# Row maxima of an attention block: the elementwise output goes back over the PSUM columns that were read

## The chip, the cores and the metric

The kernel runs on one core of a Trainium2 chip. The metric is the device time of one execution in microseconds; lower is better. A core has five engines with a queue each: TensorE (PE in the profile; its weight loads are PEld), VectorE (DVE), ScalarE (ACT), GpSimd (POOL) and SyncE (SP), which here only issues transfers. Each engine works through its own queue in order and waits on semaphores where it needs another's result, or, as will matter here, its own.

## The reference

Four layers in a row, A B A B, on a sequence of 2048 tokens of width 640. Each adds to `x` the output of an attention with 32 heads of 20 columns, taken of the layer-normalized `x`. A is linear attention. B cuts the sequence into four segments of 512 and mixes a causal softmax inside each segment with a memory of the segments before:

```
def _B_ref(x, wq, wk, wv, wo, beta):
    ...
    for s in range(N):                       # N = 4 segments of L = 512
        qs, ks, vs = q[:, :, s], k[:, :, s], v[:, :, s]
        logits = jnp.einsum("bhqd,bhkd->bhqk", qs, ks) * scale + mask
        p = _softmax(logits, axis=-1)
        a_dot = jnp.einsum("bhqk,bhkd->bhqd", p, vs)
        pq = phi(qs)
        num = jnp.einsum("bhld,bhde->bhle", pq, M)
        den = jnp.einsum("bhld,bhd->bhl", pq, z)[..., None] + 1e-6
        o = g * (num / den) + (1.0 - g) * a_dot
        ...
```

The softmax needs the maximum of each row of the masked logits. That maximum is what the changed line computes.

## The kernel before

Two streams of work are woven together: the dense one (layer norms, transposes, projections with split 16-bit weights, the linear attention and the memory) and the attention of the B layers. A planner with rough costs decides in which order their pieces are emitted. TensorE's queue keeps that order exactly (it is the one engine in `MANUAL`); the queues of the others are put in order by the scheduler of the language, from the same emission order and from what it takes to be ready.

The attention of a B layer goes by groups of four heads: eight groups in a segment, four segments, two layers, so 64 groups. Each group runs through three stretches (`STRETCHES`), in which work on the new group is interleaved with the group before and the one before that. What bears on the change:

- `stacks` loads the queries and keys of the group (lines 994 and the like).
- `row_max` (lines 997 to 1016) makes the logits a second time, only for their maxima. For each entry of `MAXES` it takes two PSUM banks, one for each half (`par`) of the partitions that hold the heads, lets TensorE write the products into them (line 1008), and then reduces them on VectorE (line 1015). There are five entries for a group, so 320 pairs of banks in all and 16 maxima for a group, 1024 in all. Three of the five entries hold two pieces of columns: 384 and 128 twice, and 256 and 256 once; two hold one piece of 512.
- Line 1015 is one instruction for the maximum, which adds a 16-bit mask (`maskw`) to the products and takes the largest sum of each row. It has two outputs: the sums themselves, elementwise, which nobody reads, and the maximum, which comes into `mg` by a second instruction that reads the accumulator out. In the profile the first is CUSTOM_DVE_ANT_0 and the second DVE_READ_ACCUMULATOR2_ANT, both at L1015.
- The elementwise output goes into `junk`, a 16-bit tile of 512 columns in SBUF with one buffer, so all 1024 maxima write the same memory.
- `split_max` (lines 1024 and 1025) turns the 16 maxima of a group into a sum of two 16-bit numbers, TensorE transposes these (line 1033), ScalarE copies them (line 1035), and a transfer writes them as two further rows of the queries (line 1038). They are subtracted by the matmul of the scores.
- `scores` (line 1050) makes the logits again, transposed and with the maxima taken off, and ScalarE takes their exponential (line 1054); GpSimd zeroes the triangle (line 1061); `weigh` (line 1077) multiplies with the values, and `normalize` (lines 1090 to 1101) divides.

The eight PSUM banks are taken in turn by everything that TensorE makes (`bank`, tag `ps`, 8 buffers). A bank is given out again when its last reader is done. So a matmul of whichever kind can wait for a maximum, through the bank that the maximum still reads. Other lines that the prediction names: 325 and 330 (transposes and the copy of their low part), 387 and 401 (projections), 428 (a sum of two SBUF tiles), 465 (the memory's quotient), 545 (a running sum), 885 and 893 (the memory's update), 1093 and 1100 (the reciprocal and the product of `normalize`).

Of the kernel before, what the change touches and what calls it, by code (L numbers as in the profile page):

```python
# [23 lines left out]
SEG = 512  # L24
# [118 lines left out]
class Kernel:  # L143
# [855 lines left out]
    def row_max(self, G, todo):  # L999

        nc, bp, qs, ks = self.nc, self.bp, G["qs"], G["ks"]
        bs = [self.bank() for _ in range(2)]
        cost = 0
        for p, i, a in todo:
            n = (i + 1) * P
            for par in range(2):
                r = slice(64 * par, 64 * par + 60)
                nc.tensor.matmul(bs[par][:, a:a + n], qs[r, p, i * P:(i + 1) * P], ks[r, p, :n],  # L1008
                                 start=True, stop=True)
                cost += n * COL  # L1010
        for par in range(2):
            for p, i, a in todo:
                n = (i + 1) * P
                junk = bp.tile([P, SEG], BF16, tag="junk", name="junk", bufs=1)
                nc.vector.tensor_tensor_reduce(junk[:, :n], bs[par][:, a:a + n], self.maskw[:, SEG - n:],  # L1015
                                               1.0, NEG, OP.add, OP.max, G["mg"][:, par, p, i:i + 1])
        return cost

# [346 lines left out]
```

## Time and profile before

| | us |
|---|---|
| median of 3 runs | 1751.35 |
| lowest and highest of them | 1750.96, 1752.2 |
| span of the profiled execution | 1750.1 |
| VectorE busy in it | 1195.0 |
| of that, line 1015 | 499.3 |
| TensorE busy in it (modelled ends) | 1674.0 |

The span goes from the first to the last instruction of one execution. The profile says nothing of what lies around it; the median of the runs is 1.25 us longer. Busy time of TensorE is an upper reading, since the ends of its pipelined matmuls are modelled. A group of instructions is named by its source line, engine, operation and out<-in by the program's names; then come the shapes, the count, the busy time, the mean in ns, and the idle time of its engine in front of it with what ended it.

### The profile page before, as it was taken

Reading aid. Unit: us, or ns where it says so; the run is one execution under the profiler, and the core shown is the slowest. Engines: PE = TensorE matmul, PEld = TensorE weight load, DVE = VectorE, ACT = ScalarE, POOL = GpSimd, SP = SyncE. Lnnn points to the kernel's source line nnn. Section 1 sums busy time; section 2 is a strip of 40 time slices with the busy share of each in tenths; the row PEclk is TensorE's granted clock in tenths of the full one; section 3 lists DMA queues with packets and bytes.
Section 4 is the critical chain, followed back from the end, with each engine's and each line's share of the span. In section 5 each row is a group of like instructions: output and inputs, shape, how many; then the busy total and the mean of one; then the engine's idle time right before and its main releaser. Section 6 shows DMA issues by size and latency. Waiting matters only on the chain.

```text
span 1750.1 us, 36310 instructions
## 1 busy us (share of the span) xinstructions
PE 1674.0 (96%) x13032; PEld 1045.6 (60%) x13032; DVE 1195.0 (68%) x3856; ACT 970.3 (55%) x1818; POOL 519.0 (30%) x982
## 2 busy tenths in 40 slices
PE   6999999999999999999989999999999999999998
PEld 4676666654665566456556777566446545644555
DVE  8645534577787677768864456746888877878773
ACT  5545433357557546667665553333675575666674
POOL 1543350022123312433342211221421432233452
PEclk9999999999999999999999999999999999999999
DMA  7422453422322322361211303433232323223332
GB/s 263 180 109 94 151 187 107 135 70 90 109 69 82 107 86 81 123 204 53 77 43 44 109 31 121 169 103 114 74 106 79 111 80 107 92 82 109 126 118 91
DMA packets 118332, 187.60 MB, mean 107 GB/s; under 512 B 13948, under 2 KB 79612, under 8 KB 115848
## 3 DMA queue, kind: packets, MB, share of 16 engines
q1 hardware_dynamic: 105896, 142.68, 25.2%
q0 software_dynamic: 3040, 21.63, 3.5%
q10 hardware_dynamic: 9216, 20.98, 3.1%
q8 instruction: 103, 1.69, 0.4%
q14 instruction: 77, 0.63, 0.1%
HBM read 106.05 MB, written 78.64 MB: 106 GB/s over the span
## 4 chain that ended last, share of the span: by engine, by line
PE 73%; DVE 13%; ACT 6%; issue 3%; POOL 2%; DMA 2%; SPq 0%; ACTq 0%; DVEq 0%; POOLq 0%
PE ps L401 31%; PE ps L387 16%; PE ps L1077 6%; DVE junk L1015 4%; PE ps L1050 3%; PE ps L325 3%; PE ps L1008 3%; ACT pe L1054 3%; PE ps L566 3%; PE ps L456 3%; PE ps L893 1%; PE ps L1090 1%; PE ps L732 1%; DVE st L344 1%; DVE oT L330 1%
## 5 line engine op out<-in xcount | busy, mean ns | idle before, releaser
L1015 DVE CUSTOM_DVE_ANT_0 junk<-ps,maskw 128x512 bf16<-128x512 f32 (+3 forms) x1024 | 499.3, 488 | 90.5 <-PE ps L1008 30.1
L1054 ACT ACTIVATE pe<-ps,lsc 128x512 f32<-128x512 f32 x640 | 394.6, 694 | 95.9 <-PE ps L1050 92.4
L1061 POOL TENSOR_SCALAR_AFFINE_SELECT pe<-pe 128x256 f32<-128x256 f32 (+1 forms) x640 | 229.7, 366 | 446.5 <-ACT pe L1054 442.0
L401 PEld LDWEIGHTS <-xT 128*128 128x128 f16 x2880 | 280.6, 98 | 114.9 <-issue 10.9
L401 PEld LDWEIGHTS <-oT 128*128 128x128 f16 x1920 | 185.5, 98 | 80.0 <-issue 6.9
L1077 PE MATMUL ps<-pe,v 128*32 128x512 f32 (+3 forms) x2048 | 161.5, 439 | 8.0 <-POOL pe L1061 3.3
L401 PE MATMUL ps<-w_Bo,oT 128*128 128x320 f16 x960 | 141.9, 301 | 1.5 <-ACT pe L1054 0.9
L387 PE MATMUL ps<-xT,w_Bq 128*128 128x512 f16 x600 | 140.1, 379 | 1.7 <-ACT pe L1054 0.8
L1008 PE MATMUL ps<-ks,qs 60*128 60x512 f16 (+3 forms) x1024 | 129.0, 299 | 12.2 <-DVE mg L1015 3.4
L401 PE MATMUL ps<-w_Bv,xT 128*128 128x320 f16 x960 | 139.7, 299 | 0.7 <-ACT v L434 0.7
L387 PE MATMUL ps<-xT,w_Bk 128*128 128x512 f16 x600 | 138.8, 379 | 1.1 <-DVE mg L1015 0.5
L401 PE MATMUL ps<-w_Ak,xT 128*128 128x320 f16 x960 | 136.1, 299 | 0.5 <-ACT r L415 0.5
L1050 PE MATMUL ps<-qs,ks 62*128 62x512 f16 (+3 forms) x1024 | 106.5, 300 | 3.3 <-ACT pe L1054 1.5
L858 DVE SCALAR_TENSOR_TENSOR nat<-ps,nat 128x512 f16<-128x512 f32 x80 | 54.9, 687 | 77.6 <-ACT nat L857 77.5
L427 POOL TENSOR_SCALAR e<-e 128x320 f32<-128x320 f32 (+1 forms) x52 | 82.4, 1584 | 83.4 <-ACT e L423 79.2
L1077 PEld LDWEIGHTS ps<-pe,v 128*32 128x32 f32 x2048 | 63.6, 110 | 65.7 <-issue 43.5
L1008 PEld LDWEIGHTS <-qs 60*128 60x128 f16 x1024 | 50.8, 94 | 82.5 <-issue 55.1
L857 ACT ACTIVATE nat<-ps 128x512 f16<-128x512 f32 x80 | 48.2, 602 | 93.6 <-PE ps L387 73.3
L387 PEld LDWEIGHTS <-w_Bk 128*128 128x128 f16 x600 | 57.4, 98 | 65.2 <-issue 5.3
L387 PEld LDWEIGHTS <-w_Bq 128*128 128x128 f16 x600 | 56.8, 98 | 65.7 <-issue 7.6
L349 POOL TENSOR_TENSOR rs<-rs,mhalf 128x1 f32<-128x1 f32 x48 | 28.3, 590 | 223.8 <-DVE rs L348 215.6
L479 POOL TENSOR_TENSOR xn<-xn,xo 128x320 f32<-128x320 f32 x56 | 48.5, 869 | 139.4 <-ACT xn L478 134.6
(220 smaller groups left out, 2671.9 us busy)
## 6 DMA issues: line engine op xcount, KB each, us to landing
x<-xn ACTq DMA_DIRECT2D x48, 320.0 KB
qs<-qd SPq DMA_DIRECT2D x128, 120.0 KB
ks<-kd SPq DMA_DIRECT2D x128, 120.0 KB
xo<-x SPq DMA_DIRECT2D x48, 320.0 KB
pqi<-pqd SPq DMA_DIRECT2D x32, 320.0 KB
qd<-nat SPq DMA_DIRECT2D x40, 256.0 KB
kd<-nat SPq DMA_DIRECT2D x40, 256.0 KB
x<-in_A_x SPq DMA_DIRECT2D x16, 320.0 KB
```

The costliest lines, as they stand in the source:

```text
L325: nc.tensor.transpose(pt[:, (c - c0) * P:(c - c0 + 1) * P], src[:, c * P:(c + 1) * P], self.ident)
L387: nc.tensor.matmul(p, w[:, c, a, t * P:(t + 1) * P], xT[:, c, b, :], start=k == 0, stop=k == 3 * C - 1)
L401: nc.tensor.matmul(p, xT[:, c, a, i * P:(i + 1) * P], w[:, c, b, n * HN:(n + 1) * HN], start=k == 0, stop=k == 3 * C - 1)
L427: nc.gpsimd.tensor_scalar(e, e, 1.0, eps, op0=OP.min, op1=OP.add)
L456: nc.tensor.matmul(nd[:, lo - k * cut:hi - k * cut], pq[t], mem[:, OFF[t] + lo - a:OFF[t] + hi - a], start=first, stop=True, skip_group_ch ...
L858: nc.vector.scalar_tensor_tensor(nat[:, 1], p, QK_SHIFT, nat[:, 0], op0=OP.mult, op1=OP.subtract)
L1008: nc.tensor.matmul(bs[par][:, a:a + n], qs[r, p, i * P:(i + 1) * P], ks[r, p, :n], start=True, stop=True)
L1015: nc.vector.tensor_tensor_reduce(junk[:, :n], bs[par][:, a:a + n], self.maskw[:, SEG - n:], 1.0, NEG, OP.add, OP.max, G["mg"][:, par, p, i ...
L1050: nc.tensor.matmul(b[:, a:a + n], ks[r, p, j * P:(j + 1) * P], qs[r, p, j * P:], start=True, stop=True)
L1054: nc.scalar.activation(e, b, AF.Exp, scale=self.lsc)
L1061: nc.gpsimd.affine_select(d, d, pattern=pat, compare_op=OP.is_ge, fill=0.0, base=0, channel_multiplier=-1)
L1077: nc.tensor.matmul(G["pv"][32 * h4:32 * h4 + 32, j * P:], v[j][:, h * E1:h * E1 + 32], G.pop((p, par, j)), start=j == 0, stop=j == 2, skip ...
```

## The change

The elementwise output of the maximum goes into the PSUM columns that the instruction reads, as 32-bit, instead of into `junk`, which is no longer used. Nothing reads those columns afterwards. Counts, shapes, mask and maxima stay.

```
             for p, i, a in todo:
                 n = (i + 1) * P
                 junk = bp.tile([P, SEG], BF16, tag="junk", name="junk", bufs=1)
-                nc.vector.tensor_tensor_reduce(junk[:, :n], bs[par][:, a:a + n], self.maskw[:, SEG - n:],
+                nc.vector.tensor_tensor_reduce(bs[par][:, a:a + n], bs[par][:, a:a + n], self.maskw[:, SEG - n:],
                                                1.0, NEG, OP.add, OP.max, G["mg"][:, par, p, i:i + 1])
```

More of the change, by code (lines that the diff above doesn't have):

```diff
@@ L1014, in row_max @@
                 junk = bp.tile([P, SEG], BF16, tag="junk", name="junk", bufs=1)
-                nc.vector.tensor_tensor_reduce(junk[:, :n], bs[par][:, a:a + n], self.maskw[:, SEG - n:],
+                nc.vector.tensor_tensor_reduce(bs[par][:, a:a + n], bs[par][:, a:a + n], self.maskw[:, SEG - n:],
                                                1.0, NEG, OP.add, OP.max, G["mg"][:, par, p, i:i + 1])
```

## The prediction

> **What bounds the kernel now.** I read the engine shares of the page first, then the chain that ended last, then the groups by form, then the timeline of VectorE, and last who waits for the maxima. In the page, the columns are busy time, share of the span and instructions; below it stands the chain by engine, and the two groups of the maxima and the exponentials.
>
> ```profile
> span 1750.1 us, 36310 instructions
> ...
> PE 1674.0 (96%) x13032; PEld 1045.6 (60%) x13032; DVE 1195.0 (68%) x3856; ACT 970.3 (55%) x1818; POOL 519.0 (30%) x982
> ...
> PE 73%; DVE 13%; ACT 6%; issue 3%; POOL 2%; DMA 2%; SPq 0%; ACTq 0%; DVEq 0%; POOLq 0%
> ...
> L1015 DVE CUSTOM_DVE_ANT_0 junk<-ps,maskw 128x512 bf16<-128x512 f32 (+3 forms) x1024 | 499.3, 488 | 90.5 <-PE ps L1008 30.1
> L1054 ACT ACTIVATE pe<-ps,lsc 128x512 f32<-128x512 f32 x640 | 394.6, 694 | 95.9 <-PE ps L1050 92.4
> ```
>
> TensorE leads, but not alone: the chain spends 13% of the span, some 230 us, in VectorE. The line of the maxima is the costliest group of the page and has 4.3% of the chain, 75 us, which the chain in order of time says by line:
>
> ```profile
> by line: PE ps L401 31.0%; PE ps L387 15.7%; PE ps L1077 6.4%; DVE junk L1015 4.3%; PE ps L1050 3.4%; PE ps L325 3.2%; PE ps L1008 3.1%; ACT pe L1054 2.9%; issue 2.9%; PE ps L566 2.7%; PE ps L456 2.7%; PE ps L893 1.4%; PE ps L1090 1.1%; PE
> ```
>
> At 488 ns each, 75 us are 154 of the 1024 maxima; the other 870 run beside TensorE. Windows of the attention (columns: length, busy time and instructions of each engine, granted clock, DMA) tell how full VectorE is there:
>
> ```profile
> 340.00:930.00 590.00, 567.36 (x4685) 343.68 (x4685) 447.47 (x1615) 363.63 (x677) 176.15 (x398) 1.00 0.28 91
> 1190.00:1715.00 525.00, 500.30 (x4147) 287.17 (x4147) 410.13 (x1476) 326.96 (x598) 174.98 (x381) 0.99 0.31 99
> ```
>
> VectorE is busy 858 of these 1115 us (77%), before its own waiting is counted. The clock is full, so nothing here is the throttle's.
>
> **What the change removes: waits of VectorE for itself.** Each row maximum is two instructions, the maximum and an 83 ns readout of its accumulator. All maxima write the one scratch tile, so that each has to wait until the one before it has finished, its readout included. The timeline shows what this costs (start, length, instruction):
>
> ```profile
> 721.12 0.56 DVE L1015 CUSTOM_DVE_ANT_0 junk<-ps,maskw 128x384 bf16<-128x384 f32 x1
> 721.60 0.08 DVE L1015 DVE_READ_ACCUMULATOR2_ANT mg<- 128x1 f32 x1
> 721.72 0.29 DVE L1015 CUSTOM_DVE_ANT_0 junk<-ps,maskw 128x128 bf16<-128x128 f32 x1
> 721.94 0.08 DVE L1015 DVE_READ_ACCUMULATOR2_ANT mg<- 128x1 f32 x1
> 722.16 0.56 DVE L1015 CUSTOM_DVE_ANT_0 junk<-ps,maskw 128x384 bf16<-128x384 f32 x1
> 722.65 0.08 DVE L1015 DVE_READ_ACCUMULATOR2_ANT mg<- 128x1 f32 x1
> 722.76 0.29 DVE L1015 CUSTOM_DVE_ANT_0 junk<-ps,maskw 128x128 bf16<-128x128 f32 x1
> 722.98 0.08 DVE L1015 DVE_READ_ACCUMULATOR2_ANT mg<- 128x1 f32 x1
> 723.21 0.69 DVE L1015 CUSTOM_DVE_ANT_0 junk<-ps,maskw 128x512 bf16<-128x512 f32 x1
> 723.82 0.08 DVE L1015 DVE_READ_ACCUMULATOR2_ANT mg<- 128x1 f32 x1
> 724.05 0.69 DVE L1015 CUSTOM_DVE_ANT_0 junk<-ps,maskw 128x512 bf16<-128x512 f32 x1
> 724.67 0.08 DVE L1015 DVE_READ_ACCUMULATOR2_ANT mg<- 128x1 f32 x1
> 724.67 0.25 DVE L1093 RECIPROCAL rc<-ps 128x16 f32<-128x16 f32 x1
> 724.95 0.49 DVE L1100 TENSOR_TENSOR tmp<-ps,rc 128x320 f32<-128x320 f32 x1
> ...
> 725.59 0.52 PE L325 MATMUL ps<-ident,otok 128*128 128x128 f32 x3 [0.41 <-DVE tmp L1100]
> ```
>
> Three cadences, from the start of a readout to the start of what follows. A reciprocal that waits for nothing recent starts with the readout: 0.00 (724.67). A maximum that waits for this readout alone: 0.11 to 0.12 (721.60, 722.65). A maximum that waits for the readout and also for a new PSUM bank: 0.22 to 0.23 (721.94, 722.98, 723.82), because the second wait needs a separate semaphore instruction, which then stands behind the first. At 725.59 TensorE pays for such a run: it waits for a copy that stands behind six maxima.
>
> The rows that group them:
>
> ```profile
> L1015 DVE DVE_READ_ACCUMULATOR2_ANT mg<- x1024: 76/83/88, 340.1 to 1708.5; 128x1 f32 x171
> L1015 DVEq EVENT_SEMAPHORE  x453: 21/21/21, 346.4 to 1707.6; - x151
> ...
> who waited for it (us, times):
>   PEld ps L325: 4.3, 17
>   PEld L1050: 3.5, 9
>   PE ps L1008: 3.4, 10
> ...
>   PEld ps L893: 1.1, 2
>   PEld L1033: 1.1, 4
>   PE ps L401: 0.8, 2
>   PE ps L387: 0.8, 2
>   PEld ps L885: 0.7, 1
>   PE ps L893: 0.5, 1
> ```
>
> Counted along the whole timeline, 356 maxima have the long cadence behind a readout and 292 the short one; the other 376 stand behind another kind of instruction and lose nothing. To start with the readout instead saves 0.227 and 0.117 us (the exact medians are gaps of 144, 34 and -83 ns from the readout's end).
>
> The changed program, built, says how many waits go. PE's order is the same in all rows. On VectorE 885 maxima carried a wait for VectorE before, 648 of them for the readout directly in front; now 466 do, and only 8 for the one in front. The rest look two or three readouts back, which are done. A pair of banks now reads:
>
> ```
> L1015 ISA ps,mg<-ps,maskw 128x384 [waits PE_49]
> L1015 ISA mg 128x1
> L1015 ISA ps,mg<-ps,maskw 128x384 [waits PE_49]
> L1015 ISA mg 128x1
> L1015 ISA ps,mg<-ps,maskw 128x128 [waits DVE_49]
> L1015 ISA mg 128x1
> L1015 ISA ps,mg<-ps,maskw 128x128 [waits DVE_49]
> ```
>
> Gain on VectorE: 356 x 0.227 + 284 x 0.117 = 81 + 33 = 114 us, or 0.111 us per maximum. On the path only the maxima of the chain count: 154 x 0.111 = 17.1 us. The second reading agrees: the waits of TensorE that a maximum ended add up to 16.2 us in the list above (POOL's left out), in some 50 stalls of 0.3 us, each behind a run of maxima that gets shorter by more than that.
>
> The Trainium skill speaks against this ("VectorE: DVE Perf Modes", The DRAIN you can't avoid): eight copies with a semaphore after each took as long as with one after the last, "the semaphore costs nothing extra here". By that the sum would be zero and the time 1751. The trace does not agree: 0.11 and 0.23 us against 0.00.
>
> **What it adds: order inside a pair of banks.** Three of five pairs in a group hold two parts, 192 in all. VectorE took both parts of the first bank, then both of the second; now the banks alternate, as quoted. By the rows from 721.12 on, the first bank came free after 0.90 us (722.02) and the second after 1.94 (723.06). Without gaps it is 0.48 + 0.48 + 0.22 + 0.08 = 1.26 for the first and 1.48 for the second: 0.36 later, 0.46 earlier. Of some 50 stalls about 15 can hang on such a first bank, at most 5 us; since each earlier pair left VectorE earlier by about as much, I take 2.
>
> **What it adds: the write goes to PSUM as 32-bit.** No VectorE instruction of this kernel writes PSUM, so no row has the price. The nearest are 128x320 instructions with the operands elsewhere:
>
> ```profile
> L465 DVE TENSOR_TENSOR otok<-ps,rc 128x320 f32<-128x320 f32 x48 | 23.3, 488 | 0.4
> L428 DVE TENSOR_TENSOR pk<-e,r 128x320 f32<-128x320 f32 x32 | 15.7, 491 | 35.2 <-POOL e L427 33.9 <-ACT e L423 1.2
> L545 DVE TENSOR_TENSOR z<-z,e 128x320 f32<-128x320 f32 x30 | 15.6, 521 | 0.7
> ```
>
> A first operand in PSUM instead of SBUF is 3 ns cheaper (488, 491); the dearest row is 33 ns above the first. So -3 to +33 ns each; on the chain, 154 times that is 0 to +5 us. I take 0, since PSUM as such does not show in 488 against 491.
>
> **What it moves.** ScalarE, GpSimd and SyncE keep their work; a few normalizations, selects and loads change places with a neighbour, mostly by one exponential, 0.69 us each by the L1054 row. They move both ways; I take 0, and 3 us either way into the range.
>
> **Sum.** -17 + 2 + 0 + 0 = -15 us against the profiled 1750.1, which is 1.25 us under the median of the runs, 1751.35. Forecast: **1736 us**.
>
> **Rivals.**
> *Larger gain, chance 0.12.* The split of the maxima follows the last one of a group, and its consumer waits too, as the list for the tile of the maxima says (its row for the transposes' loads, then its row for the transposes):
>
> ```profile
>   PEld L1033: 15.2, 21
>   PE pm L1033: 4.6, 2
> ```
>
> Were these 20 us gone with the 16, the time would be 1751 - 36 = 1715.
>
> *The write costs more, chance 0.12.* Between 33 and 97 ns each the gain shrinks from 10 us to nothing: 1741 to 1751. The Trainium skill has such a price ("Perfetto Trace Analysis", Optimizing Scalar/DVE Operations): some 60 ns of access overhead on SBUF, 125 on PSUM. By it, 65 ns x 154 = 10 us, an estimate, would leave 1746. The rows of 488 and 491 ns do not show it for reads; no run here shows a write.
>
> *Another wait takes its place, chance 0.10.* Where TensorE no longer waits for maxima it waits for an exponential that was nearly as late: ScalarE is 62% busy in the two windows. For it: line 1054 has 2.9% of the chain. Against: ScalarE itself sat idle 92 us before these for TensorE. Time 1750.
>
> *Slower, chance 0.09.* Reading and writing one bank take turns, so that an element needs two steps. The forms' step is (0.69 - 0.29)/384 = 1.04 ns per element by the timeline; another such step on 320 elements, the mean of 512, 384, 128 and 256 in equal numbers, adds 333 ns. Less the 111 saved that is 222 x 154 = 34 us, plus the 2: 1787. The sign turns at 97 ns each (15 us over 154). Against: a 32-bit write of 0.96 elements per ns is no more than the reading that runs there now.
>
> The forecast as such, gain 9 to 21 us, keeps 0.57.
>
> **Numbers.** Two runs of this kernel differ by some 0.2%, 3.5 us; that bounds "same". Faster: 0.57 + 0.12 + 0.09 of the dearer write = 0.78. Same: 0.09 of the third rival and 0.03 of the second, 0.12. Slower: 0.09 and 0.01 of the third, 0.10. The range goes from the larger gain with a little movement, 1714, to the third rival, 1750; it leaves out the slower case and about a tenth besides.
>
> **What would show it.** Right: maxima that follow a readout start with it (0.00), the semaphore rows at line 1015 fall from 453 to 168, a 128x512 maximum stays at 0.69 us, the waits of TensorE for a maximum halve, and the line's share of the chain falls below 4%. The first step is wrong if 0.11 stays; the write's price is wrong if a 512-column maximum takes over 0.72 us, and the sign if it takes over 0.80; the sum is wrong if VectorE gains its 114 us and TensorE's stalls move to ScalarE.

## The result, and the profile after

The changed kernel takes 1744.6 us (median of 9 runs, 1742.69 to 1745.8) against 1751.15 before on the same chip (9 runs, 1747.26 to 1752.2). The ratio is 0.9963 [0.9954, 0.9973]: a gain of 6.5 us, where 15 were forecast. The profiled execution has a span of 1741.4 us, 8.7 less than that of before. In what follows, "before" and "after" also name the two kernels.

The page of the changed kernel: span, engines, chain by engine, the maxima and their readouts.

```profile
span 1741.4 us, 36031 instructions
...
PE 1668.7 (96%) x13032; PEld 1048.4 (60%) x13032; DVE 1183.8 (68%) x3856; ACT 969.3 (56%) x1818; POOL 518.7 (30%) x982
...
PE 77%; DVE 10%; ACT 6%; issue 2%; POOL 2%; DMA 2%; SPq 0%; ACTq 0%; POOLq 0%; DVEq 0%
...
L1015 DVE CUSTOM_DVE_ANT_0 ps<-ps,maskw 128x512 f32<-128x512 f32 (+3 forms) x1024 | 472.8, 520 | 40.4 <-PE ps L1008 38.1
...
L1015 DVE DVE_READ_ACCUMULATOR2_ANT mg<- 128x1 f32 x1024 | 144.7, 141 | 0.0
```

VectorE's part of the chain falls from 13% to 10%, and the chain by line says that the maxima's own part falls from 4.3% to 1.6% (75 to 28 us):

```profile
by line: PE ps L401 31.7%; PE ps L387 16.9%; PE ps L1077 7.5%; PE ps L1050 3.7%; PE ps L1008 3.4%; ACT pe L1054 3.3%; PE ps L325 3.2%; PE ps L566 2.8%; PE ps L456 2.7%; issue 2.4%; DVE ps L1015 1.6%; PE ps L1090 1.4%; PE ps L893 1.4%; PE ps
```

The timeline of VectorE shows two maxima of 512 and the run of four that the prediction quoted:

```profile
717.17 0.69 DVE L1015 CUSTOM_DVE_ANT_0 ps<-ps,maskw 128x512 f32<-128x512 f32 x1
717.78 0.14 DVE L1015 DVE_READ_ACCUMULATOR2_ANT mg<- 128x1 f32 x1
717.78 0.73 DVE L1015 CUSTOM_DVE_ANT_0 ps<-ps,maskw 128x512 f32<-128x512 f32 x1
718.43 0.14 DVE L1015 DVE_READ_ACCUMULATOR2_ANT mg<- 128x1 f32 x1
718.43 0.60 DVE L1015 CUSTOM_DVE_ANT_0 ps<-ps,maskw 128x384 f32<-128x384 f32 x1
718.94 0.14 DVE L1015 DVE_READ_ACCUMULATOR2_ANT mg<- 128x1 f32 x1
718.94 0.60 DVE L1015 CUSTOM_DVE_ANT_0 ps<-ps,maskw 128x384 f32<-128x384 f32 x1
719.46 0.14 DVE L1015 DVE_READ_ACCUMULATOR2_ANT mg<- 128x1 f32 x1
719.46 0.33 DVE L1015 CUSTOM_DVE_ANT_0 ps<-ps,maskw 128x128 f32<-128x128 f32 x1
719.71 0.14 DVE L1015 DVE_READ_ACCUMULATOR2_ANT mg<- 128x1 f32 x1
719.71 0.33 DVE L1015 CUSTOM_DVE_ANT_0 ps<-ps,maskw 128x128 f32<-128x128 f32 x1
719.96 0.14 DVE L1015 DVE_READ_ACCUMULATOR2_ANT mg<- 128x1 f32 x1
```

A maximum now starts together with the readout in front of it (717.78 and 717.78): 0.00, as forecast. But the readout takes 0.14 instead of 0.08 us, and a maximum behind one is longer: 0.73 behind, 0.69 where it stands alone. Its readout comes 0.65 us after its start (717.78 to 718.43) where it was 0.61 to 0.62 (723.21 to 723.82). The run of four takes 1.67 us from its start to the start of its last readout plus 0.14 (718.43 to 720.10); it took 1.94.

Who waited for the maxima's line:

```profile
L1015 DVEq EVENT_SEMAPHORE  x168: 21/21/50, 378.4 to 1698.0; - x168
...
who waited for it (us, times):
  PEld L1050: 3.2, 8
  PEld L1033: 1.4, 5
  PEld ps L456: 1.1, 5
  PE ps L1050: 0.9, 2
  PEld ps L325: 0.9, 4
  PEld ps L885: 0.9, 4
  PE ps L1008: 0.6, 2
  PEld ps L893: 0.2, 1
```

The semaphore rows fall from 453 to 168. The listed waits of TensorE add up to 9.2 us, where they were 16.2. Among the waits of TensorE by what ended them, these rows of the two kernels moved most besides, except for the waits at the split's transposes, which a later section shows (engine, line, releaser, total us, times, longest). Before:

```profile
PEld L1008 <- issue: 55.1, 132, 0.9
...
PEld ps L1077 <- POOL pe L1061: 18.1, 49, 1.8
```

After:

```profile
PEld L1008 <- issue: 47.7, 121, 1.4
...
PEld ps L1077 <- POOL pe L1061: 24.6, 56, 2.3
```

TensorE's weight loads stand less at the maxima's own products (line 1008; "issue" names no releaser) and longer at line 1077 for GpSimd's zeroing of the triangle.

### The profile page after: what moved, and what is told of

It is laid out like the page before. It is cut to its first block, busy times and chain, and to the rows that moved or that the text cites. A ratio compares the mean times of both kernels' runs of the same rounds, so it can differ in the third digit from the quotient of the medians.

```text
span 1741.4 us, 36031 instructions
## 1 busy us (share of the span) xinstructions
PE 1668.7 (96%) x13032; PEld 1048.4 (60%) x13032; DVE 1183.8 (68%) x3856; ACT 969.3 (56%) x1818; POOL 518.7 (30%) x982
## 4 chain that ended last, share of the span: by engine, by line
PE 77%; DVE 10%; ACT 6%; issue 2%; POOL 2%; DMA 2%; SPq 0%; ACTq 0%; POOLq 0%; DVEq 0%
PE ps L401 32%; PE ps L387 17%; PE ps L1077 8%; PE ps L1050 4%; PE ps L1008 3%; ACT pe L1054 3%; PE ps L325 3%; PE ps L566 3%; PE ps L456 3%; DVE ps L1015 2%; PE ps L1090 1%; PE ps L893 1%; PE ps L732 1%; DVE st L344 1%; DVE oT L330 1%
## 5 line engine op out<-in xcount | busy, mean ns | idle before, releaser
L1015 DVE CUSTOM_DVE_ANT_0 ps<-ps,maskw 128x512 f32<-128x512 f32 (+3 forms) x1024 | 472.8, 520 | 40.4 <-PE ps L1008 38.1
L1015 DVE DVE_READ_ACCUMULATOR2_ANT mg<- 128x1 f32 x1024 | 144.7, 141 | 0.0
L1008 PE MATMUL ps<-ks,qs 60*128 60x512 f16 (+3 forms) x1024 | 124.6, 297 | 8.9 <-ACT pe L1054 3.2
L1008 PEld LDWEIGHTS <-qs 60*128 60x128 f16 x1024 | 50.3, 94 | 75.0 <-issue 47.7
L349 POOL TENSOR_TENSOR rs<-rs,mhalf 128x1 f32<-128x1 f32 x48 | 27.6, 576 | 218.7 <-DVE rs L348 218.7
```

The costliest lines, as they stand in the source:

```text
L1015: nc.vector.tensor_tensor_reduce(bs[par][:, a:a + n], bs[par][:, a:a + n], self.maskw[:, SEG - n:], 1.0, NEG, OP.add, OP.max, G["mg"][:, p ...
```

## The experiments

Four theories for the missing 8.5 us. A: the write to PSUM costs what the prediction took as nothing. B: a microsecond of VectorE's time is worth less than the chain's share says, since other work is nearly as late; its price would fall as VectorE gets emptier. C: the alternating order inside a pair costs. D: GpSimd's zeroing, which line 1077 now waits longer for, hides the gain. Where a kernel's name does not say what it starts from: e1, e2 and e8 are edits of before, e3 is after again, e4 and e11 are edits of after. The runs of before on each experiment's chip are those of its table row.

| kernel | median us (range) | before there | ratio to before |
|---|---|---|---|
| e1_sbuf_turns | 1741.38 (1740.14 to 1743.15) | 1750.69 | 0.9947 [0.9936, 0.9959] |
| e2_sbuf_banks | 1743.02 (1742.46 to 1744.61) | 1750.69 | 0.9957 [0.9945, 0.9969] |
| e3_again | 1743.99 (1743.09 to 1745.73) | 1750.69 | 0.9963 [0.9951, 0.9975] |
| e4_narrow | 1736.71 (1735.53 to 1741.0) | 1750.69 | 0.9925 [0.9913, 0.9937] |
| e5_before_nosel | 1740.82 (1737.96 to 1741.64) | 1750.43 | 0.9941 [0.9929, 0.9954] |
| e6_after_nosel | 1731.98 (1728.04 to 1732.71) | 1750.43 | 0.9895 [0.988, 0.991] |
| e7_before_more | 1779.51 (1779.2 to 1780.09) | 1750.43 | 1.0166 [1.0152, 1.018] |
| e8_f32_sbuf | 1788.97 (one run) | 1750.43 | |
| e9_after_more | 1758.56 (1754.88 to 1758.93) | 1752.14 | 1.0035 [1.0023, 1.0048] |
| e10_before_half_more | 1771.76 (1769.35 to 1775.04) | 1752.14 | 1.0117 [1.0103, 1.013] |
| e11_narrow_nosel | 1722.43 (1721.22 to 1724.09) | 1752.14 | 0.9835 [0.9822, 0.9849] |
| e12_before_nine | 1792.88 (1790.03 to 1795.11) | 1752.14 | 1.0235 [1.0221, 1.0249] |

**The same removal without the write, in both orders.** The waits go and the banks alternate as in after, but the output stays in SBUF (two 8-bit tiles, in the room of the one 16-bit tile):

```
-        for par in range(2):
-            for p, i, a in todo:
+        for p, i, a in todo:
+            for par in range(2):
-                junk = bp.tile([P, SEG], BF16, tag="junk", name="junk", bufs=1)
+                junk = bp.tile([P, SEG], mybir.dt.uint8, tag="junk", name="junk", bufs=2)
```

> The elementwise output stays in SBUF, as 8-bit numbers in two scratch tiles that take turns (SBUF has room for no more), and the two banks of a pair alternate as in the changed kernel; the queues of TensorE, ScalarE, GpSimd and SyncE are the changed kernel's, VectorE's but for some 50 places. So the waits of VectorE for itself are gone and nothing is written to PSUM. Theory A (the write to PSUM has a price that the prediction left out: in the changed kernel a readout takes 141 ns instead of 83 and a maximum behind a readout starts its own readout some 0.04 us later): readouts of 83 ns, a 512-column maximum 0.61 us from its start to its readout, and a time near the prediction, 1735 to 1739 beside 1751 for the kernel before and 1744.6 for the changed one. Theory B (what VectorE gains beyond the first half is lost to other waits of TensorE): the same 83 ns, but 1742 to 1745. An 8-bit write that is dearer than a 16-bit one would show as maxima longer than 0.69 us at 512 columns.

The second kernel has only the last line of this, so its banks come one after the other as before:

> The same two scratch tiles in SBUF, but the maxima of a pair in the order of the kernel before: both parts of the first bank, then both of the second. Theory C (the first bank of a pair comes free later in the changed kernel, by up to 0.36 us, and this costs): 2 to 5 us below the run whose banks alternate. Theories A and B have no word on the order: within 1 us of that run.

And the changed kernel beside them:

> The changed kernel once more, beside the others on one chip: 6 to 7 us below the kernel before, 1743 to 1746.

Measured: 1741.4, 1743.0 and 1744.0. The first lies between what theory A (1735 to 1739) and theory B (1742 to 1745) expected. The groups by form of the first kernel have the readout and the two ends of the sizes:

```profile
L1015 DVE CUSTOM_DVE_ANT_0 junk<-ps,maskw 128x512 uint8<-128x512 f32 x256 | 167.0, 685 | 20.3 <-PE ps L1008 20.0
...
L1015 DVE DVE_READ_ACCUMULATOR2_ANT mg<- 128x1 f32 x1024 | 84.5, 83 | 0.0
L1015 DVE CUSTOM_DVE_ANT_0 junk<-ps,maskw 128x128 uint8<-128x128 f32 x256 | 63.7, 285 | 0.0
```

In after the same forms read:

```profile
L1015 DVE CUSTOM_DVE_ANT_0 ps<-ps,maskw 128x512 f32<-128x512 f32 x256 | 174.0, 714 | 13.3 <-PE ps L1008 11.9
...
L1015 DVE CUSTOM_DVE_ANT_0 ps<-ps,maskw 128x128 f32<-128x128 f32 x256 | 74.6, 327 | 0.1
```

So the write costs 29 to 42 ns per maximum and 58 per readout, and in time the difference of the first and the third kernel, about 2.6 us: small, but their runs hardly overlap (1740.1 to 1743.2 against 1743.1 to 1745.7). Even without it the removal brings 9.3 us, not 15. Theory C finds no support: the alternating order is 1.6 us better, not worse, with runs that overlap.

**Maxima over the last 128 columns only**, in after. All 1024 become short; the maxima are then not those of the rows.

```
-... bs[par][:, a:a + n], bs[par][:, a:a + n], self.maskw[:, SEG - n:],
+... bs[par][:, a + n - P:a + n], bs[par][:, a + n - P:a + n], self.maskw[:, SEG - P:],
```

> The changed kernel with maxima over the last 128 columns of each piece alone, so that the subtracted row maxima are not those of the whole row. By the rows by form (714, 588, 452 and 327 ns) this takes another 199 us from VectorE, at the same count of instructions and waits. Theory A (VectorE's time at the maxima still sets a good part of the end): 1725 to 1735. Theory B (TensorE is held by others already): 1740 or more, and the waits of TensorE for a maximum near zero.

1736.7: VectorE's busy time falls by 187 us more (1183.8 to 997.0), the time by 7.3, or 0.04 us for each. That lies between theory A (1725 to 1735) and theory B (1740 or more): the maxima still cost some time, but little for what they occupy.

**Without GpSimd's zeroing**, before and after (the triangle is then not zeroed):

```
-        nc.gpsimd.affine_select(d, d, pattern=pat, compare_op=OP.is_ge, fill=0.0, base=0,
-                                channel_multiplier=-1)
```

> The kernel before without GpSimd's zeroing of the triangle (640 instructions; the future tokens then stay in the softmax); the other four queues keep their order to the instruction. It is the base for the next run. Theory D (after the change TensorE waits for the zeroing instead: its waits for it rose from 18.1 to 24.6 us at the weight loads of line 1077): a few us below the kernel before. Theory B (no single wait takes over, the stalls spread): the same, a few us.

> The changed kernel without the zeroing of the triangle, beside the run of the kernel before without it. Theory D: the change now brings clearly more than the 6.7 us that it brings with the zeroing, 10 us or more between these two. Theory B: 5 to 8 us between these two.

1740.8 and 1732.0: without the zeroing the change brings 8.8 us instead of 6.5, between the two expectations (5 to 8, 10 or more). By this GpSimd's zeroing hid some 2 of the missing 8.5 us. The runs of the two kernels spread over 3.7 and 4.7 us, so even these 2 are not resolved, and D is a small part at most.

**More maxima, before.** Each 128-column maximum is made twice; results stay.

```
-            for p, i, a in todo:
+            for p, i, a in [x for t in todo for x in [t] * (2 if t[1] == 0 else 1)]:
```

> The kernel before with each 128-column maximum made twice, 256 more maxima with their readouts and their waits for VectorE itself, by the rows of before some 0.35 to 0.45 us each and so 90 to 115 us more of VectorE: as much as the change was to take away. If the share of the chain (154 of 1024) is the price of a maximum in both directions, 14 to 17 us more: 1764 to 1768. If the price falls with VectorE's load, as the first runs have it (0.08 us per us for the first 114 us, 0.04 for the next 199), it is dearer on this side still: 12 us or more. If it is even, 0.08 each way: 7 to 9 us.

1779.5, 29.1 us more. In its timeline a second maximum begins 0.33 us after the first:

```profile
731.79 0.29 DVE L1015 CUSTOM_DVE_ANT_0 junk<-ps,maskw 128x128 bf16<-128x128 f32 x1
732.00 0.08 DVE L1015 DVE_READ_ACCUMULATOR2_ANT mg<- 128x1 f32 x1
732.12 0.29 DVE L1015 CUSTOM_DVE_ANT_0 junk<-ps,maskw 128x128 bf16<-128x128 f32 x1
```

That is about twice what the chain's share gave (14 to 17 us). 256 x 0.33 = 85 us of VectorE cost 0.34 each, while the 114 us that e1 takes away bring 9.3 / 114 = 0.08 each. The two sides of before are not alike.

**Is 32-bit the write's price?** Before, with a 32-bit scratch tile; to make room for it in SBUF, the exponentials' tile has nine buffers instead of ten.

```
-                junk = bp.tile([P, SEG], BF16, tag="junk", name="junk", bufs=1)
+                junk = bp.tile([P, SEG], F32, tag="junk", name="junk", bufs=1)
-PE_BUFS = 10
+PE_BUFS = 9
```

> The kernel before with a 32-bit scratch tile in SBUF (still one, still waited for), and nine buffers instead of ten for the exponentials to make room. For the durations alone: a readout of 83 ns if the 141 of the changed kernel come from PSUM, 141 if they come from the 32-bit write; a 512-column maximum of 0.69 us in either case.

Its groups by form show 83 and 687 ns as before, so the longer readout and maximum of after do not come with 32 bits. They come with the write to PSUM; no run writes PSUM columns other than those it reads, so what writing in place adds is not separated.

```profile
L1015 DVE CUSTOM_DVE_ANT_0 junk<-ps,maskw 128x512 f32<-128x512 f32 x256 | 175.9, 687 | 29.4 <-PE ps L1008 8.9
...
L1015 DVE DVE_READ_ACCUMULATOR2_ANT mg<- 128x1 f32 x1024 | 84.8, 83 | 0.0
```

The time of 1789 had to be told apart by before with the nine buffers alone (the second pair of lines):

> Before with nine instead of ten buffers for the exponentials, the scratch tile unchanged. If the nine buffers were what made the kernel with the 32-bit scratch tile slow, it stands near that one's 1789, 30 to 42 us above before, and TensorE waits for GpSimd's zeroing at line 1077 some 20 us. If it was the 32-bit write, 1750.

1792.9. The nine buffers alone make the kernel that slow: TensorE's wait at line 1077 for GpSimd grows from 18.1 to 58.0 us.

```profile
PEld ps L1077 <- POOL pe L1061: 58.0, 96, 4.2
...
PE ps L1077 <- POOL pe L1061: 20.3, 26, 3.7
```

**More maxima, after.** The same doubling in after:

> After, with each 128-column maximum made twice: 256 more maxima in VectorE, at 0.30 us from one to the next about 77 us, which is most of what the change had removed. If VectorE's total is what counts, with a price that rises with its load (theory B), the time comes back to near that of before: 4 to 6 us above after, 1748 to 1750. If each microsecond more costs what the doubling cost before (0.29 to 0.39 us, the price of a full VectorE), it is 22 to 30 us above after, 1766 to 1774, and the gain of the change was small for another reason than a flat price. If the price stays flat (0.08 us per us as between before and the output in SBUF), 6 us.

1758.6, 6.4 us above before and, by the two differences to before, 13 above after. In a run of after a 128-column maximum takes 0.25 us (719.46 to 719.71), not the 0.30 expected, so 64 us of VectorE cost 0.20 each: the expected 4 to 6 us and 22 to 30 us are both wrong, and so are the 6 of an even price. Given back, the time costs more than its removal had brought.

**Half the doubling, before:**

```
+            for p, i, a in [x for t in todo for x in [t] * (2 if t[:2] == (0, 0) else 1)]:
```

> Before, with half as many maxima doubled (the 128-column ones of the first of two p: 128 more instead of 256). If the price is one straight line above before, half of 29.1 us: 14 to 15 us above before, 1765. If it rises with the load, less than half, 7 to 12 us. By the chain's share of before (154 of 1024 maxima) some 7 to 8.

1771.8: 19.6 us for half of the extra maxima, where all of them cost 29.1. Every expectation was below that. So theory B is wrong in its form: the price does not rise evenly with VectorE's load. It depends on where the extra time falls, as the end of this section shows.

**Narrow maxima without the zeroing**, both cuts in after:

> After with the maxima over the last 128 columns only and without GpSimd's zeroing of the triangle (both leave out work, so the output differs). After without the zeroing was 12.0 us under after, narrow maxima 7.3 us. If VectorE's maxima and GpSimd's zeroing bind in different places, the two add up: 1744 - 19.3 = 1724.7. If they hide each other, more: under 1720. If TensorE's own work is the floor that both run against, less: 1727 or above.

1722.4, between two of the expectations (1724.7 if the two add up, under 1720 if they hide each other): 22.2 us below after if 1744.6 is taken, where the two alone give 19.3. They nearly add up; neither hides much of the other.

**What follows the time.** One row moves with the time in all kernels in which only the maxima differ: the weight loads of line 1008 that stand still under "issue". For e7 and e10:

```profile
PEld L1008 <- issue: 82.7, 180, 1.4
```

```profile
PEld L1008 <- issue: 77.5, 167, 1.9
```

In the last row of the table the times of two chips are compared, each as its difference to before.

| against | kernel | that row, us | its change | change of the time |
|---|---|---|---|---|
| before (55.1) | after | 47.7 | -7.4 | -6.5 |
| | e1_sbuf_turns | 46.2 | -8.9 | -9.3 |
| | e2_sbuf_banks | 46.8 | -8.3 | -7.7 |
| | e4_narrow | 38.4 | -16.7 | -14.0 |
| | e9_after_more | 58.2 | +3.1 | +6.4 |
| | e10_before_half_more | 77.5 | +22.4 | +19.6 |
| | e7_before_more | 82.7 | +27.6 | +29.1 |
| e5_before_nosel (56.8) | e6_after_nosel | 46.9 | -9.9 | -8.8 |
| e6_after_nosel (46.9) | e11_narrow_nosel | 37.8 | -9.1 | -11.3 |

What such a wait looks like in before (timeline of TensorE and of the maxima's readout):

```profile
724.22 0.10 PEld L1008 LDWEIGHTS <-qs 60*128 60x128 f16 x2
724.44 0.74 PE L1008 MATMUL ps<-ks,qs 60*128 60x384 f16 x4
724.67 0.08 DVE L1015 DVE_READ_ACCUMULATOR2_ANT mg<- 128x1 f32 x1
724.81 0.10 PEld L1008 LDWEIGHTS <-qs 60*128 60x128 f16 x2 [0.49 <-issue]
```

The second pair of loads stands still for 0.49 us and goes on 0.06 us after a readout has ended. The list names no releaser for the loads, but the trace has one for the product that starts with them at 724.80: its semaphore was set by this readout at 724.76, 0.04 us earlier. Of the stalls in this row, the table counts those that end in the same way, 0.035 to 0.055 us after the semaphore of a maximum's readout. Its last column adds up, over the 64 groups, the time from the first to the last product of the fourth entry of `MAXES`:

| kernel | stalls in the row | of them behind a maximum | us of these | fourth entry, first to last product, us |
|---|---|---|---|---|
| before | 132 | 31 | 13.6 | 20.7 |
| after | 121 | 7 | 1.9 | 14.1 |
| e1_sbuf_turns | 117 | 6 | 2.1 | 13.8 |
| e10_before_half_more | 167 | 62 | 31.8 | 31.8 |
| e7_before_more | 180 | 71 | 34.4 | 30.7 |

The commonest such stall, 12 of the 31 before and 29 and 30 in e10 and e7, is the one quoted: the second bank of a group's fourth entry waits for the second maximum of its third entry. After and e1 have none there. It also tells in large part why half of the extra maxima costs most of the whole: those of e10 are made at the second entry, so they stand in VectorE's queue ahead of the third entry's maxima, and the fourth entry's products take 11 us longer (of the 19.6 in the time); the further ones of e7 are made at the fourth entry itself, too late to hold it up more. In after the row falls by less (7.4 us) than its stalls behind maxima (11.7), so other stalls grew: there, too, other work was nearly as late.

## Why the prediction was right or wrong

- **The waits removed: right.** The cadence is 0.00, the semaphore rows fell to 168. The rule on semaphores that cost nothing ("VectorE: DVE Perf Modes", The DRAIN you can't avoid, of the Trainium skill) does not hold here: a maximum that waited for the readout directly in front started 0.11 to 0.23 us after it, and 0.00 without the wait; with these waits gone, and without the write, the time fell by 9.3 us.
- **The write: taken at 0, wrong.** The bound of 0.72 us for a 512-column maximum was passed behind a readout (0.73), and the readout, which the prediction did not price at all, went from 83 to 141 ns. The nearest rows were reads of PSUM (488 against 491 ns), and they said nothing of a write. From one maximum to the next it is some 40 ns, just above the range's upper end of 33, and in time about 2.6 us. The Trainium skill's price ("Perfetto Trace Analysis", Optimizing Scalar/DVE Operations), by an estimate from its 60 and 125 ns 65 more on PSUM than on SBUF, is near the 58 that the readout gained. That the 1746 worked out from it came near 1744.6 is luck: it takes 10 us for the write, where 2.6 were measured, from a removal worth 17, where 9.3 were measured.
- **The order in a pair: taken as a cost of 2 us, not seen.** e1 against e2 gives a gain of 1.6 us, not resolved.
- **The sum: the step that failed.** 154 x 0.111 = 17.1 us charged each maximum of the chain the full saving, and the second reading let all 16.2 us of TensorE's waits go. Without the write the removal brought 9.3 us (e1). The text itself expected these waits to halve, and they did, by 7.0 us (16.2 to 9.2); a halving in the sum would have given 8. Of the 8.5 us that are missing, this term makes 7.8 (17.1 less 9.3) and the write 2.6; the 2 us charged for the order, which were not seen, go the other way. The chain's share is what would be saved if nothing else were as late. One rival is separated by no run: VectorE's queue also came out in another order. By their starts in the traces, 169 of its 1808 other instructions stand behind one to seven more maxima after than before, 18 behind fewer; e1 and e2 have nearly the order of after, so their 9.3 and 7.7 us include whatever this costs. The prediction spoke of places that change on the other engines only. The wait at the split's transposes, 20 us before, fell to 6.2 in after (rows below, from the list of the maxima's tile; the prediction shows those of before) without the time following: the larger gain of 1715 is refuted, although the waits that it named did shrink.

```profile
  PEld L1033: 4.7, 9
...
  PE pm L1033: 1.5, 1
```

- **The rivals.** The time landed where the dearer write and the replaced wait had been put (1741 to 1751), inside the range, but by two terms together: about 2.6 us from the write, the rest from the chain's price being too high. The wait that took the place is GpSimd's zeroing more than the exponential: the line 1077 row rose by 6.5 us, of which e5 and e6 show some 2 in the time, not resolved. The slower case, that reading and writing one bank takes turns, is refuted: a 512-column maximum grew by 27 ns in the mean, not by hundreds.
- **What stays open.** How much the other order of VectorE's queue costs, and which of the waits that took the place of those for maxima hold back how much of the 17 us.

## What to carry to other kernels

In this case the share of the chain lay above what a removal gave (17 us against 9.3) and below what an addition cost (14 to 17 us against 29.1): 114 us of VectorE taken away were worth 0.08 each, 42 to 85 us added to before 0.34 to 0.47 each. Where the text says that waits will halve, let the sum say half. Look at how long the waiting engine stands in the loop around the change, the unnamed part too: one such row at line 1008 followed the time through nine comparisons, and the products beside its loads name what they waited for.

## What was not expected of the hardware

- A maximum whose elementwise output goes to the PSUM columns it reads makes the readout behind it longer, 141 against 83 ns, though the readout itself writes 128x1 into SBUF; with 8-, 16- and 32-bit outputs in SBUF it stays 83.
- One buffer fewer for the exponentials (nine for ten) costs 40.7 us, 1792.9 against 1752.1, more than any doubling of maxima tried.
